# Rounding copies of weight sums on GpSimd instead of ScalarE, in a fused attention and feed-forward kernel

## The chip, the cores and the metric

The kernel runs on one core of one Trainium2 chip. The metric is the device time of one execution in microseconds (us), median of three runs. In the rows below PE is TensorE's matmul stream and PEld its weight loads, DVE is VectorE, ACT is ScalarE, POOL is GpSimd, and SP issues DMAs. A name such as L273 is a line of the kernel file.

## What is computed

```python
scores = scale * np.matmul(q, k.transpose(0, 1, 3, 2)) - np.log(S)
attn = 1.0 / (1.0 + np.exp(-scores))
x = np.matmul(attn, v)            # (8, 12, 448, 64) -> 3584 tokens x 768
h = x @ w_in                      # 768 x 2048
g = s * np.maximum(h, 0.0)**2 + b
out = g @ w_out                   # 2048 x 768
```

The two weight matrices arrive as 64-bit floating point numbers and are turned into 32-bit ones in the kernel.

## The kernel before

A matmul operand of full precision is kept as two parts: `hi`, the value rounded to the format fp32r, and `lo`, the rest, also in fp32r. A product is then the sum of three matmuls (hi·hi, hi·lo, lo·hi, the table `PARTS`). To make the parts, one instruction copies the raw values into a tile of type fp32r (this rounds), and a second one, always on DVE at L198, subtracts the copy from the raw values.

The program has three stages, which follow one another on PE.

**Attention, 0 to about 246 us.** 24 steps (8 batches x 3 groups of four heads), called quads. In quad n PE computes the scores (L459, with the parts `qkh` and `qkl` of q and k), the products with v (L495, L504) and a small piece of the next quad's scores (L481). ACT makes the sigmoids (L434, L436), and the rounded part `qkh` of the next quad (L412). DVE copies results from PSUM (L512), and near the end of its list for a quad it makes `qkl` of the next quad (L198, `qkl<-qk,qkh`). Beside this, a plan with a place for every quad converts weight blocks: DVE and ACT together turn a 128x768 block of 64-bit words into `wf` (L219 on DVE, L223 on ACT, then L225, L228, L232, L235 on DVE).

Also by plan, the attention makes sums of w_out blocks for d_ff pairs 0 to 3. `sums_out` uses three functions that `sums_ops` returns: `make(g)` adds and subtracts blocks on DVE into the raw half of a tile `t` (L195, L198), `hi(g)` copies the raw half rounded into the other half (L273), and `lo(g)` makes the rest (L198, `t<-t`) and stores the tile to DRAM. The table `SUMS_AT` gives the quads of make, hi and lo. Within a quad DVE takes conversions first, then make and lo, then the first step of the next conversion (L219), then `qkl`.

**Token block 0, about 246 to 370 us.** The first 512 tokens go through both weight matrices without sums, in 16 steps: 18 matmuls with a block of w_in (L606), 18 with a block of w_out (L811). In a step ACT rounds two weight blocks (L331), DVE makes their rest (L198, `w<-wf,w`), and ACT and DVE make the activations `g` (L800 to L803 on ACT, L198 `g<-r,g` on DVE). At the same time the generator `sums` makes the sums of w_in blocks for all 8 pairs, with the same functions of `sums_ops`: three tiles for each pair.

**The other six blocks of 512 tokens, from 370 us.** They are computed in two groups of three with the stored sums (L1137, L1269). Later sums of w_out have functions of their own there (L933).

The tile framework keeps each engine's instructions in the order in which the program issues them (`manual_schedule`), so the order on each engine is that of the Python code. GpSimd has no work in this kernel but four memsets of constants at the start.

Of the kernel before, what the change touches and what calls it, by code (L numbers as in the profile page):

```python
# [102 lines left out]
def sigmoid_attention_relu2_ffn(  # L103
# [10 lines left out]
    nc = tc.nc  # L114
# [67 lines left out]
    def f32(ap):  # L182
        return ap.bitcast(F32)
# [13 lines left out]
    def sub(o, x, y):  # L197
        nc.vector.tensor_tensor(o, x, y, op=ALU.subtract)  # L198
# [39 lines left out]
    def block(l, f, n):  # L238

        third, hf = (int(n[0]), int(n[1])) if l == 0 else (int(n[1]), int(n[0]))  # L240
        return wf[l][f + hf * NP][:, third]

    def op(o, x, sign, y):
        (add if sign > 0 else sub)(o, x, y)

    def sums_ops(l, f, tl):

        raw, ts = {}, {}

        def val(n):  # L250
            return raw[n] if n in raw else block(l, f, n)

        def make(g):
            t = ts[g] = tl.tile([P, 3, 2, KW], F32R, name=f"t_{l}_{f}_{g}")
            k = 0
            for n, x, sign, y in SUMS[l][g]:
                if len(n) == 2:
                    raw[n] = f32(t[:, k : k + 2, 1])
                    raw[n[0]], raw[n[1]] = f32(t[:, k, 1]), f32(t[:, k + 1, 1])
                    two = raw[y] if len(y) == 2 else raw[y].unsqueeze(1).to_broadcast([P, 2, KW])  # L260
                    h, b0 = int(x[0]), int(x[1])
                    op(raw[n], wf[l][f + h * NP][:, b0 : b0 + 2], sign, two)
                    k += 2
                    continue
                if n == "t":
                    raw[n] = f32(t[:, 0, 0])
                else:
                    raw[n] = f32(t[:, k, 1])
                    k += 1
                op(raw[n], val(x), sign, val(y))  # L270

        def hi(g):
            nc.scalar.copy(ts[g][:, :, 0], f32(ts[g][:, :, 1]))  # L273

        def lo(g):
            t = ts[g]
            sub(t[:, :, 1], f32(t[:, :, 1]), f32(t[:, :, 0]))

            def store():
                nc.sync.dma_start(  # L280
                    wd[l][f // 2][:, 3 * g : 3 * g + 3, f % 2],
                    f32(t).rearrange("p k h c -> p k (h c)"),
                )
                tl.free(t)

            if l:
                stores.append(store)
            else:
                store()

        return make, hi, lo

    def sums(l, f, tl):

        make, hi, lo = sums_ops(l, f, tl)
        make(0)
        make(1)
        yield
        hi(0)
        hi(1)  # L300
        yield
        make(2)
        lo(0)
        lo(1)
        yield
        hi(2)
        yield
        lo(2)
        yield
# [487 lines left out]
    def activate(f, ph):  # L797
        g = gp.tile([P, 2, TB], F32R, tag="g", name=f"g_{f}")
        r = rt.tile([P, TB], F32, tag="r", name=f"r_{f}")
        nc.scalar.activation(r, ph, AF.Relu)  # L800
        nc.scalar.activation(r, r, AF.Square)
        nc.scalar.activation(r, r, AF.Identity, bias=b_sb, scale=s_sb)
        nc.scalar.copy(g[:, 0], r)  # L803
        sub(g[:, 1], r, f32(g[:, 0]))
        return g
# [15 lines left out]
    ts = [sums(0, k, cx) for k in range(NP)]  # L821
# [3 lines left out]
    for i, f in enumerate(order):  # L825
# [14 lines left out]
        g = activate(f, ph)  # L840
# [151 lines left out]
    for n, blocks in enumerate(threes):  # L992
# [261 lines left out]
        for j, (i, p) in enumerate(L2):  # L1254
# [5 lines left out]
            g = gc.pop(j)  # L1260
# [81 lines left out]
```

## Time and profile before

| | |
|---|---|
| time, median of 3 runs | 997.33 us (996.52 to 997.5) |
| profiled execution | span 995.0 us from first to last instruction; no time of its own is listed apart from the span |
| PE busy | 991.2 us |
| DVE busy | 840.6 us |
| ACT busy | 616.1 us |
| POOL busy | 0.2 us |
| attention | 0 to 246 us, a quad every 9.99 us |
| token block 0 | 246 to 370 us, a step every 7.77 us |

The busy time of an engine is the time in which it executes instructions; an idle stretch is put down to the instruction that was waited for last. PE's ends are modelled, so PE's start times say more than its busy share.

### The profile page before, as it was taken

To read this page: it belongs to the slowest core of one execution; us is meant where nothing else is said; L and a number is where in the kernel's file an instruction comes from. 1 tells how busy PE (TensorE), PEld (TensorE's weight loads), DVE (VectorE), ACT (ScalarE), POOL (GpSimd) and SP (SyncE) were. 2 spreads that over 40 slices of the span, in tenths; PEclk is the share of its full clock that TensorE was granted. 3 is DMA by queue.
4 is the path that set the end of the run, shared out by engine and by line. 5 is a ranking of instruction groups with operands and counts; after the bars stand their busy time and mean duration, and the time that the engine had idled before them with its cause. 6 is when DMAs were issued, how large, how long until landed. Compare 5 with 4: busy or idle time off the path is not lost.

```text
span 995.0 us, 13973 instructions
## 1 busy us (share of the span) xinstructions
PE 991.2 (100%) x5288; PEld 783.6 (79%) x5288; DVE 840.6 (84%) x933; ACT 616.1 (62%) x687; POOL 0.2 (0%) x4
## 2 busy tenths in 40 slices
PE   9999999999999999999999999999999999999998
PEld 4555555555888888888888888888888888888887
DVE  5999999999889976799999898996465789889787
ACT  7999999998877575575455444443455336543432
POOL 0000000000000000000000000000000000000000
PEclk9999999999999999999999999999999999999999
DMA  8788898999899999999686678978666676677773
GB/s 327 282 332 324 311 372 316 418 359 402 306 404 360 371 391 407 381 334 368 215 276 204 210 260 309 305 249 267 202 207 198 205 208 197 209 239 226 229 240 123
DMA packets 101826, 287.18 MB, mean 289 GB/s; under 512 B 10240, under 2 KB 20608, under 8 KB 101760
## 3 DMA queue, kind: packets, MB, share of 16 engines
q1 hardware_dynamic: 101472, 285.84, 81.9%
q8 instruction: 42, 0.69, 0.3%
q10 hardware_dynamic: 288, 0.46, 0.1%
q14 instruction: 24, 0.20, 0.0%
HBM read 198.18 MB, written 88.08 MB: 288 GB/s over the span
## 4 chain that ended last, share of the span: by engine, by line
PE 100%; DVE 0%; issue 0%
PE o L1269 31%; PE h L1137 31%; PE pav L495 11%; PE psc L459 9%; PE po L811 6%; PE ph L606 6%; PE psc_l L481 2%; PE pav L504 2%; PE psc L465 0%; PE idle L527 0%; DVE C_t L198 0%
## 5 line engine op out<-in xcount | busy, mean ns | idle before, releaser
L1137 PE MATMUL h<-s_1h,wu 128*128 128x512 f32 x480 | 143.0, 379 | 0.0
L1137 PE MATMUL h<-s_0h,wu 128*128 128x512 f32 x480 | 143.0, 379 | 0.0
L436 ACT ACTIVATE a<-psc,nls 128x896 f32<-128x896 f32 x120 | 113.4, 1020 | 11.0 <-PE psc L459 8.3
L495 PE MATMUL pav<-a,v 128*64 128x448 f32 x576 | 113.8, 543 | 0.0
L1137 PEld LDWEIGHTS h<-s_0h,wu 128*128 128x128 f32 x480 | 90.7, 189 | 12.8
L1137 PEld LDWEIGHTS h<-s_1h,wu 128*128 128x128 f32 x480 | 90.7, 189 | 12.8
L1009 ACT COPY G<-h 128x1024 f32<-128x1024 f32 x48 | 48.9, 1019 | 82.3 <-PE h L1137 56.6
L901 ACT ACTIVATE G<-G,b_sb,s_sb 128x1024 f32<-128x1024 f32 x48 | 59.7, 1244 | 57.6 <-DVE G L898 57.0
L1137 PE MATMUL h<-s_0l,wu 128*128 128x512 f32 x240 | 91.0, 379 | 0.0
L1137 PE MATMUL h<-s_1l,wu 128*128 128x512 f32 x240 | 91.0, 379 | 0.0
L495 PEld LDWEIGHTS pav<-a,v 128*64 128x64 f32 x576 | 39.1, 137 | 62.6 <-issue 55.7
L195 DVE TENSOR_TENSOR G<-G,h 128x1024 f32<-128x1024 f32 x40 | 48.8, 1219 | 35.9 <-PE h L1137 34.7
L1269 PE MATMUL o<-g_3h,wu 128*128 128x512 f32 (+1 forms) x244 | 76.4, 376 | 0.0
L1269 PE MATMUL o<-g_0h,wu 128*128 128x512 f32 x240 | 76.3, 379 | 0.0
L1269 PE MATMUL o<-g_1h,wu 128*128 128x512 f32 x240 | 76.3, 379 | 0.0
L1269 PE MATMUL o<-g_2h,wu 128*128 128x512 f32 x240 | 76.3, 379 | 0.0
L811 PE MATMUL po<-g,w 128*128 128x512 f32 x288 | 64.8, 379 | 0.0
L811 PEld LDWEIGHTS po<-g,w 128*128 128x128 f32 x288 | 54.4, 189 | 8.0 <-DVE g L198 0.4
L606 PE MATMUL ph<-x0h,w 128*128 128x512 f32 x192 | 59.6, 380 | 0.0
L459 PE MATMUL psc<-qkh 64*128 64x448 f32 x282 | 53.8, 378 | 0.0
L198 DVE TENSOR_TENSOR qkl<-qk,qkh 128x1664 fp32r<-128x1664 f32 (+3 forms) x26 | 44.9, 1726 | 9.8 <-ACT qkh L412 9.5
L1269 PEld LDWEIGHTS o<-g_3h,wu 128*128 128x128 f32 x244 | 45.9, 189 | 6.4
(154 smaller groups left out, 2053.7 us busy)
## 6 DMA issues: line engine op xcount, KB each, us to landing
wu<-wd SPq DMA_DIRECT2D x240, 512.0 KB, 4.3
wd<-t SPq DMA_DIRECT2D x36, 768.0 KB, 8.0
qk<-qk_t SPq DMA_DIRECT2D x23, 896.0 KB, 7.2
st<-w_out SPq DMA_DIRECT2D x16, 768.0 KB, 8.6
st<-w_in SPq DMA_DIRECT2D x16, 768.0 KB, 8.6
wd<-w SPq DMA_DIRECT2D x16, 768.0 KB, 5.6
v<-v_t SPq DMA_DIRECT2D x24, 448.0 KB, 5.8
xd<-xo SPq DMA_DIRECT2D x24, 448.0 KB, 5.2
```

The costliest lines, as they stand in the source:

```text
L195: nc.vector.tensor_tensor(o, x, y, op=ALU.add)
L198: nc.vector.tensor_tensor(o, x, y, op=ALU.subtract)
L436: nc.scalar.activation(a, psc[:, :, :S], AF.Sigmoid, bias=nls, scale=SCALE)
L459: nc.tensor.matmul(o[j][:, :S], two[wi][r, i, cols], paired(two[xi][r, i, :S]), start=m == 0, stop=m == 2,)
L481: nc.tensor.matmul(psc[half[i], j, :S].rearrange("p (b a) -> p a b", a=2), x[r, i, 1, 3 * P :], x[r, i, 0, :], start=True, stop=True,)
L495: nc.tensor.matmul(pav[i][r, :S], ld_[1][:, 3 * i + c, j, :], a[i, c][:, j, :], start=c == 0, stop=False,)
L606: nc.tensor.matmul(ph, w[:, k, wi, kc * P : (kc + 1) * P], paired(x0[h][xi][:, cc, :]), start=m == 0, stop=m == 3 * NCC - 1,)
L811: nc.tensor.matmul(pos[e], w[:, k, wi, kc * P : (kc + 1) * P], paired(g[:, gi, :]), start=first and i == 0, stop=last and i == 2,)
L901: nc.scalar.activation(x, x, AF.Identity, bias=b_sb, scale=s_sb)
L1009: nc.scalar.copy(g(m, h), bk)
L1137: nc.tensor.matmul(bk[:, j], wt[:, j, wi, c * P : (c + 1) * P], paired(opd[i][xi][:, c, :]), start=i == ch[0] and m == 0, stop=m == 3 * KC ...
L1269: nc.tensor.matmul(o, wt[:, f, wi, e * P : (e + 1) * P], paired(g[gi][:, f, tk]), start=(end or i == ch[0] and p == 0) and f == 0 and m == ...
```

## The change

The function `hi` inside `sums_ops` issues its copy on GpSimd instead of ScalarE.

```diff
         def hi(g):
-            nc.scalar.copy(ts[g][:, :, 0], f32(ts[g][:, :, 1]))
+            nc.gpsimd.tensor_copy(ts[g][:, :, 0], f32(ts[g][:, :, 1]))
```

Input and output stay in SBUF, 128 partitions x 3 runs of 256 values. `sums_ops` is called from the attention (`sums_out`, 4 pairs x 3 tiles = 12 copies) and from the stage of token block 0 (`sums`, 8 pairs x 3 tiles = 24 copies). The order of PE's and of DVE's instructions stays as it was, 934 rows on DVE.

The first place is ACT in the attention, in the quads whose scores start at 26.5 us and 46.5 us (`qkh` is the rounded part of the next quad's q and k, `wf` a weight block in conversion, `t_0_0` the first sum tile of pair 0, `a` the sigmoids):

```order
 L412 CAST qkh_0_455<-qk_0_353 128x1664
 L223 ACTIVATE wf_8_106<-wf_8_106,e_bias 128x768
-L273 CAST t_0_0_395<-t_0_0_395 128x3x256
 L436 ACTIVATE a_0_l<-psc_0_l,nls 128x896
 L436 ACTIVATE a_0_0_0_516<-psc_0_0_0_509,nls 128x896
```

The copy stood behind `qkh` and the conversion and ahead of the sigmoids; it is gone from there, and nothing else moved.

The second place is ACT in the first two steps of token block 0 (`w` are the weight blocks, `ph` the first product's result, `r` the activation):

```order
 L331 CAST w_8_2832<-wf_8_105 128x3x256
 L331 CAST w_1_2863<-wf_1_108 128x3x256
-L273 CAST t_0_0_2836<-t_0_0_2836 128x3x256
-L273 CAST t_0_1_2840<-t_0_1_2840 128x3x256
 L800 ACTIVATE r_2879<-ph_2844 128x512
 L801 ACTIVATE r_2879<-r_2879 128x512
```

Two copies stood between the weight blocks and the activation; both are gone.

The third place is GpSimd's list, from the constants to the first copies of the attention (the following ones stand below these without anything between them, up to 36):

```order
 L1332 MEMSET const-bfloat16-1.0 128x1
 L1332 MEMSET const-uint8-127 128x1
-L1338 UNCONDITIONAL_BRANCH x2
+L1338 UNCONDITIONAL_BRANCH
+L273 CAST t_0_0_395<-t_0_0_395 128x3x256
+L273 CAST t_0_1_502<-t_0_1_502 128x3x256
+L273 CAST t_0_2_612<-t_0_2_612 128x3x256
+L273 CAST t_1_0_826<-t_1_0_826 128x3x256
```

The copies now stand one behind the other on an engine that has nothing else to do, each waiting for its `make` on DVE.

The fourth place is DVE, the same before and now, in the quad at 26.5 us: the rows from the `make` of `t_0_0` to the next quad.

```order
31 L198 TENSOR_TENSOR t_0_0_395<-wf_0_103,wf_8_105 128x256
32 L198 TENSOR_TENSOR t_0_0_395<-wf_0_103,t_0_0_395 128x2x256
33 L219 TENSOR_SCALAR wf_8_106<-st_8_355 128x768
34 L198 TENSOR_TENSOR qkl_0_456<-qk_0_353,qkh_0_455 128x1664
35 L512 COPY xo_2_492<-pav_2_0_466 128x448
36 L512 COPY xo_2_492<-pav_2_1_467 128x448
```

One instruction, L219, stands between the end of a `make` and `qkl`.

## Rows read from the trace of the kernel before

**Rows 1.** The page: span, busy time of each engine with its share and count, and the chain of work that ended last.

```profile
span 995.0 us, 13973 instructions
PE 991.2 (100%) x5288; PEld 783.6 (79%) x5288; DVE 840.6 (84%) x933; ACT 616.1 (62%) x687; POOL 0.2 (0%) x4
...
PE 100%; DVE 0%; issue 0%
```

**Rows 2.** Busy time of each engine by stretch: four quads of the attention, and the sum over the 23 quads from 16.54 us on. Columns: stretch, its length, PE, PEld, DVE, ACT, POOL busy (instructions), granted clock, DMA share, GB/s.

```profile
66.49:76.48 9.99, 9.99 (x78) 5.40 (x78) 9.26 (x12) 9.66 (x12) 0.00 (x0) 1.00 1.00 385
76.48:86.47 9.99, 9.99 (x78) 5.39 (x78) 9.77 (x14) 9.36 (x12) 0.00 (x0) 1.00 0.93 346
86.47:96.46 9.99, 9.99 (x78) 5.39 (x78) 9.64 (x12) 9.98 (x12) 0.00 (x0) 1.00 0.82 291
...
226.33:236.32 9.99, 9.99 (x78) 5.39 (x78) 8.77 (x10) 9.45 (x12) 0.00 (x0) 1.00 1.04 406
...
sum 229.77, PE 229.77 PEld 124.38 DVE 214.48 ACT 218.52 POOL 0.00; mean PE 9.99 PEld 5.41 DVE 9.33 ACT 9.50 POOL 0.00
```

**Rows 3.** The timeline of DVE and PE where `qkl` is late: start us, duration us, engine, line, operation [idle before, releaser].

```profile
74.49 1.89 DVE L198 TENSOR_TENSOR qkl<-qk,qkh 128x1664 fp32r<-128x1664 f32 x1 [0.48 <-ACT qkh L412]
...
76.69 0.35 PE L459 MATMUL psc<-qkl,qkh 64*128 64x448 f32 x2
...
84.15 0.57 DVE L219 TENSOR_SCALAR wf<-st 128x768 int32<-128x768 int32 x1
84.62 1.90 DVE L198 TENSOR_TENSOR qkl<-qk,qkh 128x1664 fp32r<-128x1664 f32 x1
...
86.67 0.36 PE L459 MATMUL psc<-qkl,qkh 64*128 64x448 f32 x2
...
124.62 1.89 DVE L198 TENSOR_TENSOR qkl<-qk,qkh 128x1664 fp32r<-128x1664 f32 x1 [0.33 <-ACT qkh L412]
...
126.62 0.40 PE L459 MATMUL psc<-qkl,qkh 64*128 64x448 f32 x2
126.86 0.35 PE L459 MATMUL psc<-qkh,qkl 64*128 64x448 f32 x2
127.05 0.35 PE L459 MATMUL psc<-qkh 64*128 64x448 f32 x2
```

**Rows 4.** The view of busy time by stretch, as in rows 2, for the 14 steps of token block 0 that hold the copies, and the step behind them.

```profile
253.51:362.29 108.78, 108.78 (x504) 94.95 (x504) 99.88 (x169) 79.09 (x114) 0.00 (x0) 1.00 0.96 363
362.29:370.06 7.77, 7.77 (x37) 6.80 (x37) 4.28 (x4) 3.73 (x6) 0.00 (x0) 1.00 1.06 408
```

**Rows 5.** Waits from 245 to 371 us, the stage of token block 0.

```profile
DVE g L198 <- ACT g L803: 6.9, 2, 3.5
...
DVE w L198 <- ACT w L331: 5.7, 4, 1.7
...
PEld po L811 <- DVE g L198: 0.4, 1, 0.4
```

**Rows 6.** Groups of instructions: the copies at L273, other rounding copies and the nearest other work by size, with count | busy us, mean ns | idle time before, releaser. The fourth is from the view of one line: count, then least/median/most ns.

```profile
L273 ACT CAST t<-t 128x768 fp32r<-128x768 f32 x36 | 29.4, 836 | 2.2 <-DVE t L195 1.5 <-DVE t L198 0.6
...
L901 ACT ACTIVATE G<-G,b_sb,s_sb 128x1024 f32<-128x1024 f32 x48 | 59.7, 1244 | 57.6 <-DVE G L898 57.0
...
L198 DVE TENSOR_TENSOR t<-t 128x768 fp32r<-128x768 f32 x36 | 33.4, 951 | 0.0
...
L318 DVE CAST td<-td x2: 419/420/420, 142.7 to 192.7; 128x512 fp32r<-128x512 f32 x2
...
L1332 POOL MEMSET const-float32-0.0<- 128x1 f32 x1 | 0.1, 99 | 0.2 <-issue 0.2
```

**Rows 7.** The timeline of DVE at other `make`s of the attention; the `make` ends about where L219 starts.

```profile
34.09 0.55 DVE L219 TENSOR_SCALAR wf<-st 128x768 int32<-128x768 int32 x1
34.56 1.88 DVE L198 TENSOR_TENSOR qkl<-qk,qkh 128x1664 fp32r<-128x1664 f32 x1
...
42.69 1.04 DVE L219 TENSOR_SCALAR wf<-st 128x768 int32<-128x768 int32 x2
44.54 1.89 DVE L198 TENSOR_TENSOR qkl<-qk,qkh 128x1664 fp32r<-128x1664 f32 x1 [0.81 <-ACT qkh L412]
...
53.47 0.55 DVE L219 TENSOR_SCALAR wf<-st 128x768 int32<-128x768 int32 x1
54.52 1.89 DVE L198 TENSOR_TENSOR qkl<-qk,qkh 128x1664 fp32r<-128x1664 f32 x1 [0.50 <-ACT qkh L412]
...
173.59 0.55 DVE L219 TENSOR_SCALAR wf<-st 128x768 int32<-128x768 int32 x1
174.41 1.89 DVE L198 TENSOR_TENSOR qkl<-qk,qkh 128x1664 fp32r<-128x1664 f32 x1 [0.26 <-ACT qkh L412]
...
183.48 0.55 DVE L219 TENSOR_SCALAR wf<-st 128x768 int32<-128x768 int32 x1
184.40 1.89 DVE L198 TENSOR_TENSOR qkl<-qk,qkh 128x1664 fp32r<-128x1664 f32 x1 [0.36 <-ACT qkh L412]
```

**Rows 8.** Waits over the whole span: who waited for whom, us in total, times, longest.

```profile
PEld psc L459 <- ACT t L273: 7.8, 11, 0.7
...
PEld psc L459 <- ACT wf L223: 4.9, 7, 0.7
```

**Rows 9.** Busy time of line L273 alone by stretch: a quad without a copy and one with a copy. Columns: stretch, its length, ACT busy (instructions), granted clock, DMA share, GB/s.

```profile
66.49:76.48 9.99, 0.00 (x0) 1.00 1.00 385
76.48:86.47 9.99, 0.82 (x1) 1.00 0.93 346
```

## The prediction

> **What bounds the kernel now.** I read the page's busy times and chain first: PE is busy for 991.2 of 995.0 us and the chain that ended last is PE alone [rows 1]. As PE's ends are modelled, I then looked at the stretches. A quad takes 9.99 us whether ACT has 9.98, 9.66 or 9.45 us of work in it and DVE 9.77 or 8.77 [rows 2]; a limit on ACT or DVE would have made these lengths differ. So PE sets the time, and work taken from ACT gives nothing back by itself. But DVE and ACT are close behind: 9.33 and 9.50 us of 9.99 on average. The third view, the timeline of single instructions, shows how close. PE needs `qkl` of the next quad at its second group of score matmuls. In the quad at 74.49 us `qkl` ends at 76.38 and PE takes it at 76.69. In the quad at 124.62 it ends at 126.51, PE takes it at 126.62, and the next matmul pair comes 0.24 us later instead of 0.19: PE was held by about 0.05 us [rows 3]. So PE starts 0.11 us after the end of `qkl` at the earliest, and the usual reserve is 76.69 - 76.38 - 0.11 = 0.20 us. At 84.62 it is 86.67 - 86.52 - 0.11 = 0.04 us. The reader is to see that PE is 100% busy and yet has a supplier with 0.2 us to spare.
>
> In token block 0 DVE has 99.88 us of work in 108.78 us, ACT 79.09 [rows 4]; PE waited for DVE's `g` once, by 0.4 us of weight load [rows 5].
>
> **What is removed.** 36 copies of 836 ns, 29.4 us, leave ACT [rows 6]: 12 in the attention and 24 in token block 0 (one function serves both). None of this lies on PE's path, by the equal quads. In the attention L273 stood behind `qkh`, so `qkh` does not come earlier. In token block 0 ACT's later instructions come earlier, and DVE waits less for ACT's `g` and `w` (6.9 and 5.7 us [rows 5]); that is DVE idle time, worth something only if DVE becomes the bound. Gain: 0.
>
> **What is added.** 36 copies on GpSimd. Each starts when its `make` on DVE has ended. Its result is needed by `lo`, in the attention one quad or more later, in token block 0 behind the next `make` and the weight blocks, so a copy of 1 us is not waited for. What can cost is the SBUF traffic beside DVE: nearly all DVE work in question has two operands in SBUF. No row of this trace shows GpSimd beside DVE, so I bound it: from 0 (they do not disturb each other) to full exclusion (while GpSimd copies, no such DVE instruction runs). I take exclusion for the forecast, since two-operand work is nearly all that DVE does there, and keep 0 as a rival.
>
> The Trainium skill (page "SBUF — State Buffer", section "Who interferes with whom") says that a VectorE instruction with two SBUF inputs contends with a GpSimd instruction that reads SBUF, by a lock held for the whole instruction. By that rule the exclusion is real; no run here shows it yet, and it is the rule that speaks against this change.
>
> The duration on GpSimd is unknown too; its only rows are memsets of one column, 99 ns [rows 6]. The nearest rows: DVE's rounding copy of 512 columns took 420 ns, so 0.63 us for 768; ACT's copy of the same shape 0.836; the slowest elementwise row, ACT at L901 on 1024 columns, 1.244. I take 0.84, the same instruction on the other engine, and keep 0.63 and 1.24 as ends. The page "GPSIMD Engine Reference" of the Trainium skill (section 3.1) gives 1.03 to about 1.8 cycles per element at 1.2 GHz: as an estimate 0.66 to 1.15 us for 768, and by these the sums below would be 9 and 26 us.
>
> **The attention under exclusion.** Behind each `make` stands L219, which has started before the copy can. The copy begins at L219's end, and `qkl` behind it waits. PE loses what exceeds the reserve. By quads, with 0.84:
> - At 34.56 and 84.62 `qkl` follows L219 at once [rows 3, 7]: L219 ends at 34.64, the copy at 35.48, 0.92 late, less 0.19 = 0.73; the second 0.94 less 0.04 = 0.90. Together 1.6.
> - Five quads are like 54.52, where `qkl` waits 0.5 us for `qkh` anyway [rows 7]: 54.02 + 0.84 - 54.52 = 0.34, less 0.19, about 0.16 each. Together 0.8.
> - 174.41: L219 ends at 174.14, 0.57 late, less 0.19: 0.4.
> - 184.40 has two copies behind two makes: 184.03 + 1.68 - 184.40 = 1.31, less 0.19: 1.1.
> - Two quads with a longer gap, such as 44.54 (0.81 of idle), cost nothing.
> Sum 3.9 us. With 0.63 the five fall out: 2.1. With 1.24 all pay 0.4 more: 8.6.
>
> **Token block 0 under exclusion.** Here DVE's list is dense, so I count capacity: 99.88 + 24 x 0.836 = 119.9 us of DVE and blocked DVE in a stretch of 108.78 [rows 4, 6]. The 8.9 us of idle are used up, and 11.2 us are over. DVE has worked some us ahead of PE at the end of this stretch, which would take some off; against that, not every idle moment can be used, since `g` comes from PE through ACT. I let these two cancel. DVE is next to be late: `g` and the weight blocks' `lo` reach PE late. With 0.63: 6.2 us; with 1.24: 21.0 us.
>
> From 370 us on nothing is changed.
>
> **Sum.** 3.9 + 11.2 = 15.1 us on a span of 995.0. The median of the runs lies 2.3 us above the span, which I leave as it is: 997.3 + 15.1 = 1012.4 us. With the ends: 997.3 + 8.3 = 1005.6 and 997.3 + 29.6 = 1026.9.
>
> **Rivals.**
> - No exclusion: GpSimd copies beside DVE and nothing slows. For it: no row shows the two engines disturbing each other. Against it: the dense two-operand work. Time 997.3, no change. It decides if DVE's L198 and `qkl` rows keep 951 ns and 1.89 us beside copies. Chance 0.21.
> - GpSimd is much slower, twice DVE's two-operand row of 951 ns = 1.9 us. Then each quad with a copy pays up to 1.07 more, 16.5 in the attention, and token block 0 pays 99.9 + 45.6 - 108.8 = 36.7. Time 1050. For it: no row excludes it. Against: a copy has one operand, and the copies of the same kind on two other engines take 0.63 and 0.84. Chance 0.08.
> - Faster: the wait rows name ACT's L273 as what held PE's weight loads for the scores, 11 times 0.7 us, 7.8 us in all [rows 8]. If this is a real delay of PE, it goes with the copies: 997.3 - 7.8 = 989.5. Against: the same 0.7 us stand with L223 as releaser seven times [rows 8], and the quad at 66.49, without a copy, is as long as the next one, which has one [rows 9]. It would decide if quads with copies became shorter than 9.99. Chance 0.03.
>
> **How the numbers follow.** The exclusion with a copy of 0.63 to 1.24 us has 0.68: 1005 to 1027, taken at 1012. No exclusion 0.21, slow GpSimd 0.08, faster 0.03. About 0.2% (2 us) is what a measurement tells from no change. Faster 0.03, same 0.21, slower 0.76. The range has to reach the second case, so it goes from 996.8 to 1027 and leaves out the slow copy and the gain.
>
> **What would show it.** The page: POOL busy of some 25 to 45 us in 36 copies, ACT 29 us less. Attention: `qkl` rows longer than 1.89 us or starting behind a copy in 9 or 11 quads, and these quads 10.1 to 11.1 us long while the quads without copies stay at 9.99. Token block 0: DVE's `t`, `w` and `g` rows longer than before (951 ns for `t`) or with gaps before them, the stage some 11 us longer, and PE waiting for DVE's `g` and `w` more often. After it, equal lengths in the last stage. It is wrong if the DVE rows beside copies have their old durations, if token block 0 keeps its 7.77 us a step, or if the loss sits in the attention rather than in token block 0.

## The result and the profile after

The changed kernel took 1008.11 us (median of four runs, 1007.91 to 1008.22) beside 996.92 us of the kernel before in the same session: ratio 1.0114, 95% interval [1.0099, 1.0128]. It is slower by 1.1%. The span grew from 995.0 to 1006.4 us, by 11.4 us. The forecast was 1012.4 us, with a range from 996.8 to 1027.

The page of the changed kernel, busy times and chain, answering to [rows 1]:

```profile
span 1006.4 us, 14023 instructions
PE 994.6 (99%) x5288; PEld 783.6 (78%) x5288; DVE 858.4 (85%) x933; ACT 591.0 (59%) x651; POOL 42.9 (4%) x40
...
PE 86%; DVE 10%; issue 2%; DMA 1%; ACT 1%; DVEq 0%; ACTq 0%
```

ACT is busy for 25.1 us less (not for the 29.4 us of its 36 copies, since its rows overlap a little) and GpSimd for 42.7 us more, and DVE, which has the same 933 instructions as before, is busy for 17.8 us more. The chain that ended last is no longer PE alone. Where that happened is read from the busy time by stretch. I cut it at the first score matmuls of the second quad, at the start of block 0's first L811 and near the end of its last one. First the kernel before, then the changed one:

```profile
16.47:253.34 236.87, 236.87 (x1780) 130.60 (x1777) 217.93 (x278) 222.32 (x256) 0.00 (x0) 1.00 0.91 346
253.34:370.11 116.77, 116.77 (x541) 101.94 (x540) 104.33 (x173) 83.04 (x120) 0.00 (x0) 1.00 0.96 366
```

```profile
16.15:254.11 237.96, 237.47 (x1781) 130.67 (x1777) 222.06 (x278) 214.93 (x244) 14.63 (x12) 1.00 0.92 344
254.11:381.46 127.35, 119.91 (x542) 101.08 (x541) 117.86 (x173) 65.52 (x96) 28.09 (x24) 1.00 0.88 335
```

The second number of a row is the length. The attention grew by 1.1 us, token block 0 by 10.6 us, and DVE's busy time by 4.1 and 13.5 us. The last stage is as long as before (624.9 us from the last cut to the end, both times).

In the attention four quads show where it lies:

```profile
36.13:46.59 10.46, 10.26 (x82) 5.40 (x78) 10.01 (x14) 9.45 (x12) 1.10 (x1) 1.00 0.80 300
46.59:56.57 9.98, 9.98 (x80) 5.39 (x76) 9.26 (x12) 9.18 (x11) 1.09 (x1) 1.00 0.72 261
86.53:97.08 10.55, 10.25 (x80) 5.39 (x76) 10.22 (x12) 8.96 (x11) 0.00 (x0) 1.00 0.79 284
97.08:107.07 9.99, 9.99 (x80) 5.40 (x77) 9.68 (x13) 9.45 (x12) 0.96 (x1) 1.00 1.01 381
```

Two quads are longer by 0.5 and 0.6 us, because a copy in the quad ahead of them held `qkl`. One more quad, near 177 us, grew by 0.1. The others have their old length, with a copy ahead of them or without.

Single instructions in the timeline of the changed kernel (start, duration), GpSimd first, then DVE, and last a row of DVE in the kernel before:

```profile
84.45 1.04 POOL L273 CAST t<-t 128x768 fp32r<-128x768 f32 x1 [10.06 <-issue]
...
258.06 1.35 POOL L273 CAST t<-t 128x768 fp32r<-128x768 f32 x1 [0.82 <-ACT g L803]
```

```profile
84.25 0.56 DVE L219 TENSOR_SCALAR wf<-st 128x768 int32<-128x768 int32 x1
84.71 2.52 DVE L198 TENSOR_TENSOR qkl<-qk,qkh 128x1664 fp32r<-128x1664 f32 x1
...
258.64 1.04 DVE L198 TENSOR_TENSOR t<-wf 128x256 f32<-128x256 f32 x1
```

```profile
257.38 0.42 DVE L198 TENSOR_TENSOR t<-wf 128x256 f32<-128x256 f32 x1
```

In the quad where [rows 3] had L219 at 84.15, `qkl` took 2.52 us instead of 1.90. In token block 0 a `t<-wf` of 256 columns took 1.04 us instead of 0.42. The difference is 0.62 us both times. Instruction by instruction, 23 rows of DVE in token block 0 are longer by half a microsecond or more: 16 by 0.62 or 0.63 us and 7 by 0.50 to 0.52. One of the 24 copies met none. Two groups hold 8 and 7 of these rows; their means were 951 ns [rows 6] and 953 ns before:

```profile
L198 DVE TENSOR_TENSOR t<-t 128x768 fp32r<-128x768 f32 x36 | 38.4, 1090 | 0.0
L198 DVE TENSOR_TENSOR w<-wf,w 128x768 fp32r<-128x768 f32 x32 | 34.1, 1086 | 4.4 <-ACT w L331 4.4
```

The second group has nothing to do with the tiles `t` that GpSimd copies. The copies themselves, all 36, from the view of line L273 (least, median, most ns):

```profile
L273 POOL CAST t<-t x36: 827/1109/2934, 33.9 to 370.0; 128x768 fp32r<-128x768 f32 x36
```

The one copy of token block 0 that met no DVE instruction took 0.83 us. Most that meet one are longer as well, and the longest took 2.93 us. And PE's waits for DVE in token block 0, where [rows 5] had 0.4 us once (total us, times, longest):

```profile
PEld po L811 <- DVE g L198: 9.6, 9, 1.7
...
PE po L811 <- DVE g L198: 6.3, 7, 1.3
```

### The profile page after: what moved, and what is told of

Read it like the earlier page. It is cut to its first block, busy times and chain, and to the rows that moved or that the text cites. A ratio compares the mean times of both kernels' runs of the same rounds, so it can differ in the third digit from the quotient of the medians.

```text
span 1006.4 us, 14023 instructions
## 1 busy us (share of the span) xinstructions
PE 994.6 (99%) x5288; PEld 783.6 (78%) x5288; DVE 858.4 (85%) x933; ACT 591.0 (59%) x651; POOL 42.9 (4%) x40
## 4 chain that ended last, share of the span: by engine, by line
PE 86%; DVE 10%; issue 2%; DMA 1%; ACT 1%; DVEq 0%; ACTq 0%
PE o L1269 31%; PE h L1137 31%; PE pav L495 10%; PE psc L459 8%; DVE t L198 3%; DVE w L198 2%; PE psc_l L481 2%; PE pav L504 2%; PE po L811 1%; DVE t L195 1%; DMA wd<-t 1%; PE ph L606 1%; DVE g L198 1%; DVE st L232 1%; DVE qkl L198 0%
## 5 line engine op out<-in xcount | busy, mean ns | idle before, releaser
L811 PE MATMUL po<-g,w 128*128 128x512 f32 x288 | 66.7, 383 | 6.3 <-DVE g L198 6.3
L811 PEld LDWEIGHTS po<-g,w 128*128 128x128 f32 x288 | 53.8, 189 | 16.7 <-DVE g L198 9.6
L273 POOL CAST t<-t 128x768 fp32r<-128x768 f32 x36 | 42.7, 1187 | 328.3 <-DVE t L198 157.2
```

What stands on the lines that cost most here:

```text
L273: nc.gpsimd.tensor_copy(ts[g][:, :, 0], f32(ts[g][:, :, 1]))
L811: nc.tensor.matmul(pos[e], w[:, k, wi, kc * P : (kc + 1) * P], paired(g[:, gi, :]), start=first and i == 0, stop=last and i == 2,)
```

## The experiments

Lengths of a stage are cut as above; "before" is the kernel before, run on the same chip in the same session. Two theories stood at the start. Mine: a GpSimd copy and a DVE instruction that reads two operands from SBUF exclude each other, each copy costs DVE a hold (a time in which its instruction stands still) of about 0.6 us, and the time is lost where DVE has no slack. The main rival: the rounded half now comes late, through semaphores and a slow engine, and whoever needs it waits.

**The attention alone.**

```diff
-            nc.gpsimd.tensor_copy(ts[g][:, :, 0], f32(ts[g][:, :, 1]))
+            if l:
+                nc.gpsimd.tensor_copy(ts[g][:, :, 0], f32(ts[g][:, :, 1]))
+            else:
+                nc.scalar.copy(ts[g][:, :, 0], f32(ts[g][:, :, 1]))
```

> Only the 12 copies of the attention on GpSimd, the 24 of token block 0 on ScalarE. Theory (a copy holds one two-operand DVE instruction up for about 0.6 us, and that costs PE only where it hits qkl and DVE has no gap ahead of it): about +1 us, 997.5 to 998.5, in the quads that begin near 36 and 86 us, token block 0 as long as before (116.8 us). Rival (the two stages are coupled, the loss of token block 0 comes from a DVE that leaves the attention late): +3 us or more. Rival (taking work from ScalarE pays in the attention): below 996.

Measured: 998.34 us beside 996.51, ratio 1.0016 [1.0006, 1.0026]. The attention is 238.53 us long, 1.7 more than before, and token block 0 has 116.76, as before. So the stages are not coupled. The quads near 37 and 87 us lost 0.44 and 0.55 us as in the changed kernel. A third one, near 188 us, lost 0.60 that it had not lost there. The timeline of the run shows why; `qkl` of that quad, here and then in the changed kernel:

```profile
185.33 0.56 DVE L219 TENSOR_SCALAR wf<-st 128x768 int32<-128x768 int32 x1
185.82 2.50 DVE L198 TENSOR_TENSOR qkl<-qk,qkh 128x1664 fp32r<-128x1664 f32 x1
...
185.47 1.12 POOL L274 CAST t<-t 128x768 fp32r<-128x768 f32 x1 [0.34 <-DVE t L198]
```

```profile
184.81 0.58 DVE L219 TENSOR_SCALAR wf<-st 128x768 int32<-128x768 int32 x1
185.29 1.91 DVE L198 TENSOR_TENSOR qkl<-qk,qkh 128x1664 fp32r<-128x1664 f32 x1
...
184.95 2.93 POOL L273 CAST t<-t 128x768 fp32r<-128x768 f32 x1 [0.34 <-DVE t L198]
```

Both times a copy arrived 0.14 us after the start of L219. In this run the copy got in ahead of `qkl`; in the changed kernel `qkl` went first and the copy took 2.93 us, until 0.68 us behind the end of `qkl`. One of the two waits. The program of the attention is the same in both runs, so it does not fix which one.

**Token block 0 alone** (the two branches above exchanged).

> Only the 24 copies of token block 0 on GpSimd, the 12 of the attention on ScalarE. Theory: +10.6 us over the kernel before, 1007 to 1008; attention as before, token block 0 127.4 us instead of 116.8. Rival (coupled stages): clearly less than +10.6, and the two halves don't add up to the whole change.

Measured: 1007.62 beside 996.51, ratio 1.0112 [1.0097, 1.0127]. The attention takes 236.86 us as before, token block 0 127.67, 10.9 more. The halves, 1.7 and 10.9, give 12.6 for the whole's 11.7; the difference is mostly the third quad above.

**GpSimd writes and does not read.** The 24 copies of token block 0 become memsets to zero; this leaves the rounding of these sums out.

```diff
-                nc.gpsimd.tensor_copy(ts[g][:, :, 0], f32(ts[g][:, :, 1]))
+                nc.gpsimd.memset(f32(ts[g][:, :, 0]), 0.0)
```

> In token block 0 the 24 GpSimd copies become GpSimd memsets of the same region to zero: GpSimd writes the same bytes but reads nothing (this leaves the rounding of the w_in sums out: their rounded part is zero). Attention copies on ScalarE. Theory (the two engines exclude each other on the way of reading SBUF): DVE keeps its 951 ns rows, token block 0 is 116.8 us, 997 us. Rival (they exclude each other in writing, or a GpSimd instruction as such, its semaphores and waits, makes DVE late): 1003 to 1008.

Measured: 997.33 beside 996.51, ratio 1.0007 [0.9998, 1.0017]. Stage and groups:

```profile
253.11:369.88 116.77, 116.77 (x542) 101.94 (x540) 104.61 (x173) 65.54 (x96) 15.67 (x22) 1.00 0.97 365
...
L198 DVE TENSOR_TENSOR t<-t 128x768 fp32r<-128x768 f32 x36 | 33.4, 950 | 0.0
```

GpSimd is busy for 15.67 us of a stage in which DVE works for 104.61, and DVE's `t<-t` rows keep their 950 ns. Writing the same bytes holds none of DVE's two-operand rows up. One row with a single operand is longer, a conversion's L219 that began 0.13 us behind a memset. It takes 0.69 us in the kernel before and 0.66 to 0.70 us in the other runs:

```profile
328.42 1.10 DVE L219 TENSOR_SCALAR wf<-st 128x768 int32<-128x768 int32 x1
...
328.29 0.74 POOL L276 MEMSET t<- 128x768 f32 x1 [1.48 <-DMA wd<-t]
```

Sixteen of the memsets don't wait for `make`, though (the third tile's `make` uses the rounded half as scratch), so this run alone leaves the rival alive. It shows a second thing: ACT has only 65.54 us of work here instead of 83.04, and the stage is not shorter.

**The reading without the dependency.** ACT rounds as before, and GpSimd also copies the raw half to a scratch tile (in bf16) that nobody needs.

```diff
+            nc.scalar.copy(ts[g][:, :, 0], f32(ts[g][:, :, 1]))
+            if not l:
+                nc.gpsimd.tensor_copy(scr[0], f32(ts[g][:, :, 1]))
```

> All 36 roundings on ScalarE as before; in token block 0 GpSimd copies in addition the raw half of each of the 24 tiles to a scratch tile (bf16) that nothing reads. Theory (exclusion in reading): the extra work alone costs what the change cost in token block 0, +8 to +13 us, 1005 to 1010, with DVE rows 0.5 to 0.6 us longer beside the copies. Rival (lateness of the rounded half from GpSimd is what makes lo and g late): 997, since the rounded half comes from ScalarE.

Measured: 1007.35 beside 996.51, ratio 1.0107 [1.0092, 1.0122]. Token block 0:

```profile
253.26:379.78 126.52, 119.39 (x542) 100.97 (x540) 117.86 (x173) 83.47 (x120) 27.97 (x24) 1.00 0.89 337
```

ACT has its 83 us again, nobody waits for a rounded half from GpSimd, and the stage is still 9.8 us longer, with DVE at 117.86 us, to the hundredth as in the changed kernel. One dependency is left: `lo` overwrites the raw half, so it must wait until GpSimd has read it. The traces settle what that is worth. Neither here nor in the changed kernel does the list of DVE's waits have a row for GpSimd, and here too 23 DVE rows are longer by 0.50 to 0.63 us, `w<-wf,w` among them. With the run before it this shows the cause: GpSimd's reading of SBUF beside DVE. The rival falls as the main cause. The stage is 1.15 us shorter than in the run with token block 0 alone, with as many holds; what makes up that difference is not shown.

**The copies on DVE itself**, in token block 0.

```diff
-                nc.gpsimd.tensor_copy(ts[g][:, :, 0], f32(ts[g][:, :, 1]))
+                nc.vector.tensor_copy(ts[g][:, :, 0], f32(ts[g][:, :, 1]))
```

> The 24 rounding copies of token block 0 on VectorE itself, those of the attention on ScalarE; GpSimd has nothing to do. Theory (a GpSimd copy costs DVE 0.5 to 0.63 us, about what the copy would cost DVE if it made it itself, 0.56 to 0.63 by the 420 ns row of 512 columns): DVE's work grows by 13 to 15 us as with GpSimd, token block 0 grows by 9 to 12 us, 1005 to 1009. Rival (waiting for GpSimd's result is the larger part of the loss): under +6 us, since DVE then waits for nobody. Rival (GpSimd still saves DVE something): over +14 us.

Measured: 1006.48 beside 996.64, ratio 1.0099 [1.0082, 1.0115]; the stage takes 126.63 us, 9.9 more, with 119.20 us of DVE work. As a group the copies read:

```profile
L276 DVE CAST t<-t 128x768 fp32r<-128x768 f32 x24 | 15.7, 681 | 0.0
```

So DVE made the copies itself in 14.9 us of added work, where holding still for GpSimd had cost it 13.5. Given to GpSimd, a copy still costs DVE nine tenths of its price. And with no other engine to wait for, the stage is nearly as long as in the changed kernel.

**Only the copies with a gap behind them**, 8 of the attention.

```diff
-            if l:
+            if l and (f, g) not in ((0, 0), (1, 1), (3, 1), (3, 2)):
```

> Only 8 copies of the attention on GpSimd, all but those of the two quads in which qkl follows L219 without a gap and of the quad with two copies; everything else on ScalarE. Theory (a copy behind a make is covered by DVE's wait for qkh, 0.3 to 0.8 us): no quad longer by over 0.1 us, 996.5 to 997. Rival (each copy costs about 0.15 us, as the prediction had it for five quads): five quads longer by 0.1 to 0.2 us, +0.8 us in sum; seen in the trace's quads, since the times can't tell it.

Measured: 997.06 beside 996.64, ratio 1.0003 [0.9994, 1.0013]. One quad is longer by 0.10 us, the one near 177 us, the others by nothing. Ahead of that quad the copy held a `td<-wf` by 0.62 us, and the 0.26 us for which DVE waited there [rows 7] did not cover it. A copy whose hold is covered by DVE's wait for `qkh` and the reserve of `qkl` is free.

**Each copy twice**, in token block 0.

```diff
                 nc.gpsimd.tensor_copy(ts[g][:, :, 0], f32(ts[g][:, :, 1]))
+                nc.gpsimd.tensor_copy(ts[g][:, :, 0], f32(ts[g][:, :, 1]))
```

> As the run with 24 copies of token block 0 on GpSimd, but each copy is made twice, one behind the other, into the same place. Theory (a fixed price for every copy that reads SBUF, with DVE's idle time hardly usable): 24 more holds of 0.5 to 0.63 us, +12 to +15 us on top of the +10.6, 1018 to 1023. Rival (the hold is paid once for each make, the second copy falls into idle time): 1007 to 1010.

Measured: 1020.93 beside 996.64, ratio 1.0244 [1.0228, 1.0259]. DVE's work grew by 28.4 us for 48 copies, 0.59 each: the price is per copy. The stage grew by 22.5 us, and some of that is not DVE's. PE stood still behind the first matmul of a group until 338.26 us, waiting for DVE's `g`:

```profile
334.49 0.38 PE L815 MATMUL po<-g,w 128*128 128x512 f32 x1
338.26 6.91 PE L815 MATMUL po<-g,w 128*128 128x512 f32 x17 [3.40 <-DVE g L198]
```

```profile
336.00:338.00 2.00, 0.00 (x0) 0.00 (x0) 2.00 (x3) 1.97 (x3) 1.94 (x3) 0.87 0.02 5
338.00:340.00 2.00, 1.74 (x4) 1.47 (x5) 2.00 (x3) 0.18 (x1) 1.94 (x2) 0.50 0.00 0
```

After that wait the granted clock (the third number from the end) is 0.50, the lower of its two levels, and 17 matmuls take 6.91 us where 18 took 4.05 in the kernel before.

**A third of the copies**, the third tile of each pair of token block 0.

```diff
-            if l:
+            if l or g < 2:
```

> Only the third tile of each pair in token block 0 on GpSimd, 8 copies of 24; the others and the attention on ScalarE. Capacity (the prediction's way): DVE has 8.9 us idle in the 14 steps, 8 holds of 0.6 us are 4.8 us and fit, +0 to +0.5 us, 996.5 to 997.5. Rival (idle time lies at other places than the holds, four fifths of each hold reach PE, as 10.6 of 13.5 us did): +3 to +5 us, 1000 to 1002.

Measured: 1000.32 beside 996.64, ratio 1.0035 [1.0023, 1.0047]. The stage takes 119.62 us, 2.85 more, with 109.53 us of DVE work, 5.2 more. (The profiled run took 999.41 us; the median is 3.7 us above the kernel before.) The whole stretch had room for these 5.2 us and more than half of them still reached PE. Counting capacity over the stage is wrong.

**Where the copies stand.** Two runs with six copies each, of pairs 1 and 2, and of pairs 6 and 7.

```diff
-            if l:
+            if l or f not in (1, 2):
```

> Only the 6 copies of pairs 1 and 2 of token block 0 on GpSimd, whose steps hold 1.0 to 2.2 us of idle DVE time each; all others on ScalarE. Theory (what a hold costs is decided by the idle time of its own step and the two behind it): token block 0 longer by at most 0.5 us, 996 to 997.5. Rival (a fixed share of four fifths of each hold reaches PE wherever it is): 6 x 0.56 x 0.8 = +2.7 us, 999 to 1000.

> Only the 6 copies of pairs 6 and 7 of token block 0 on GpSimd, in steps with 0.1 to 1.0 us of idle DVE time that lie ahead of the end of the stage; all others on ScalarE. Theory (place decides): +2 to +4 us, 998.5 to 1000.5, lost in the steps from about 340 us on, in DVE's g. Rival (fixed share): +2.7 us as well, and the run with pairs 1 and 2 would cost the same. Capacity over the whole stretch (the prediction's way): 0.

Measured: 997.70 beside 996.62, ratio 1.0010 [1.0000, 1.0019], for pairs 1 and 2; 998.58, ratio 1.0019 [1.0009, 1.0028], for pairs 6 and 7 (the same line with `(6, 7)`). The stage of the first, then of the second:

```profile
253.41:371.06 117.65, 117.25 (x541) 101.71 (x540) 107.34 (x173) 79.35 (x114) 6.77 (x6) 1.00 0.95 362
```

```profile
253.15:371.91 118.76, 117.80 (x541) 101.63 (x540) 107.86 (x173) 79.01 (x114) 6.84 (x6) 1.00 0.95 360
```

DVE got 3.0 and 3.5 us of added work, and the stage 0.9 and 2.0 us of length. The place decides, by a factor of about two, and the fixed share of +2.7 us is off both times. But pairs 1 and 2 were expected at +0.5 at most: their own steps absorbed the holds, and 0.2 and 0.7 us appeared behind them, in the steps that begin at 292 and 308 us. These hold no copy in this run, and DVE has 7.63 and 7.60 us of work in their 7.77 us in the kernel before. DVE's backlog travels.

## Why the prediction was right, and where it was not

- **PE sets the time and ACT's relief brings nothing.** Right. Quads with no copy ahead of them kept 9.99 us, and with the memsets ACT had 17.5 us less work in a stage of the same length.
- **Exclusion between GpSimd's copy and DVE.** Right, and the assumption that carried the sum; when it was made no row showed it. The Trainium skill's rule (page "SBUF — State Buffer", section "Who interferes with whom") agrees with the runs: a two-input DVE instruction was held up by GpSimd instructions that read SBUF (`t<-t` at 1090 ns in the mean), not by ones that only write it (950 ns).
- **The price of a copy.** The step "I take 0.84" mis-sized it. The duration was well guessed, 0.83 us undisturbed, but it is not what DVE pays. DVE's rows grew by 0.50 to 0.63 us, 13.5 us for 24 copies, 0.56 each: the copy's recorded span has parts that don't hold DVE. The same page and section of the Trainium skill say that the lock is held for the whole instruction; the rows show less than the span of one.
- **The attention, 3.9 us.** Measured 1.1. Of the quads in which `qkl` follows L219 at once, the two losses were 0.47 and 0.56, not 0.73 and 0.90, by the price. The five quads at 0.16 each cost nothing, also by the price: with 0.63 the prediction had them at nothing. The `qkl` at 174.41, taken as 0.4, cost 0.1. The quad with two copies, taken as 1.1, cost nothing in the changed kernel, since `qkl` got in ahead of the second copy, and 0.6 in the run with the attention alone. That the copy always begins behind L219 and meets `qkl` next was wrong for five of the twelve: those held another row, two an L219, two a `td<-wf` and one a `t<-wf`.
- **Token block 0, 11.2 us.** Measured 10.6, so the size is right by luck: two errors cancelled. The added work was 13.5 us, not 20.1; by the capacity count that would have been 4.6 us of loss. And the 8.9 us of idle time were not used up: over the stage DVE's idle time fell only from 12.4 to 9.5 us. The step that failed is the capacity count. The rows of DVE's waits in the changed kernel's stage say why:

```profile
DVE w L198 <- ACT w L331: 4.4, 3, 1.7
DVE t L198 <- DMA wd<-t: 1.6, 1, 1.6
DVE g L198 <- ACT g L803: 1.4, 1, 1.4
```

  Before, the same stage had 5.7 us for `w` [rows 5], 1.4 for the DMA and 3.4 for `g`. DVE still waits for the same suppliers, although it is late elsewhere; most of this idle time can't be used. The runs with pairs 1 and 2, with pairs 6 and 7 and with a third of the copies show the share that reached PE: 0.9 of 3.0, 2.0 of 3.5 and 2.85 of 5.2 us.
- **The rivals.** No exclusion fell with the longer rows of DVE in the changed kernel and with the scratch copies. The slow GpSimd fell with 0.83 us. The shorter quads did not appear.

## What to carry to other kernels

A copy moved to an idle GpSimd is not off the books if DVE works with two SBUF operands at the time: here it took 0.56 us of DVE's time, and the same copy made by DVE itself took 0.62. Before work is moved to an idle engine, look which busy engine it can hold up, and how much slack that engine has at the place of each instruction; idle time summed over a stage does not pay for it. A copy is free where the busy engine is waiting for somebody else anyway, as 7 of the 8 copies were in the run with the gaps of the attention.

## What the runs showed of the hardware beyond the forecast

One-operand work is held too: both L219 behind the `make` at 42.4 us took 1.67 us together instead of 1.04 [rows 7]. For L219 a GpSimd instruction that only writes was enough, as the one row beside a memset shows (1.10 us instead of 0.69).

```profile
42.75 1.67 DVE L219 TENSOR_SCALAR wf<-st 128x768 int32<-128x768 int32 x2
```

And a wait of PE can cost twice: in the run with doubled copies a 3.4 us wait was followed by some 6 us of matmuls at the lower clock level (0.50), about 3 us more, while the waits of the changed kernel (up to 1.3 us) left the granted clock at 1.00. Two shorter waits of the same run, 2.4 us ahead of 265.11 us and 1.9 ahead of 367.74, were followed by the lower level for 3.4 us each; one of 1.85 us, ahead of 319.06, was not.
